# Gated mix of a long convolution and an MLP mixer on one core: fewer filter matmuls, norm arithmetic on VectorE, shift copies as transfers, and another instruction order

## The chip, the core and the metric

The kernel runs on one core of one Trainium2 chip. A core has five engines that work side by side, each through its own list of instructions in a fixed order: TensorE (PE, matrix products into PSUM; its weight loads are PEld), VectorE (DVE, element by element), ScalarE (ACT, functions, and most copies out of PSUM), GpSimd (POOL, small arithmetic and the issue of accumulating transfers) and SyncE (SP, which issues most transfers). Instructions wait on semaphores for results of other engines and of transfers. The metric is the time of one execution in microseconds (us); lower is better.

## The reference

All tensors are bf16; q, k, v are 1 x 2048 x 640.

```python
x = A_q
g = sigmoid((x * gate_w).sum(-1, keepdims=True))
# a: shift convolution of k with 4 taps per channel, times v, then a causal
#    convolution over 2048 steps with the filter ssm_k (by FFT), plus kv * ssm_D, times q
kv = k_shift * v
y  = irfft(rfft(pad(kv)) * rfft(pad(ssm_k)))[:S] + kv * ssm_D
a  = q * y
# b: layernorm, w1, gelu, a shift of four channel groups by 1, -1, 2, -2 rows, w2, residual;
#    layernorm, w3 (640 -> 1536), gelu, w4 (1536 -> 640), residual
h  = gelu(layernorm(x) @ w1)
x1 = x + shifted(h) @ w2
b  = x1 + gelu(layernorm(x1) @ w3) @ w4
return g * a + (1 - g) * b
```

## The kernel before

Sequence rows are worked on in 16 tiles of 128, in four groups (`sc`) of four tiles. The long convolution is cut in four blocks of 512 steps. Each block goes to the frequency domain by a matrix product with a discrete Fourier transform that is folded by symmetry: a signal and its reverse are added and subtracted first, so that each half needs a smaller matrix.

- **Filter** (`h_load`, `h_fold`, `h_chunk`; lines 762 to 797), five chunks of 128 channels. `h_fold` has ScalarE copy the second half of a chunk backwards into `krev`, VectorE subtract and add it (two operations of 1024 elements), and two DMA transposes (issued by SyncE) turn the result into `het`. `h_chunk` multiplies with the constant `Rh` (and `Zn`, which repairs single rows): for four groups of bins `j`, with a real and an imaginary half `r`, in all 20 matmuls of 512 columns per chunk. Even bins are `j` 0 and 1, odd bins 2 and 3. ScalarE copies the results to `HF`.
- **Signal** (`kv_block`, `x_fwd`, `combine`): VectorE makes the shifted product kv, TensorE transforms it, the result lies in `XF`.
- **Products** (`unit`): VectorE multiplies `XF` and `HF` over block pairs, in operations of 2560 elements; some sums go through accumulating transfers that GpSimd issues.
- **First norm and w1** (`ln1`, `bn_math`, `mm1`): statistics on VectorE, small arithmetic on VectorE or GpSimd, the power -0.5 on GpSimd (`pool_pow`). Of the five channel groups that `mm1` yields, the last holds 32 channels of each shift group; VectorE copies them by 32 partitions to their shifted place in `hT` (line 924).
- **w2 and second norm** (`mm2`, `ln2`, `ln_math`): for each of 16 tiles, one chain of [128 x 1] operations on GpSimd with one on VectorE (lines 868 to 873). Tiles below `LNA` are normed by VectorE, the others by ScalarE. A DMA transpose follows.
- **w3, w4** (`mm3`, `mm4`, `base`): `mm4` adds its residual by an identity matmul, unless `summed` says that the tile's row is written first (`base`) and added to in DRAM.
- **End** (`final`): the inverse transform for 16 pairs of tiles, `k` 0 to 15. For `k` below `KACC` the result is added in DRAM by an accumulating transfer from GpSimd; otherwise VectorE adds the mixer's tile and SyncE writes the sum.

Every operation is recorded in program order (`Prog.op`, `Prog.dma`; `tt`, `ts`, `act`, `mm` at lines 668 to 690 are the helpers whose line numbers the profile shows). A list written out by hand, `SEQUENCE`, gives the order in which they go to their engines. `schedule` walks it with planned durations, chooses PSUM banks as it goes, and lets large loads wait for an earlier transfer when the plan has too many under way. Waits then follow from the reads and writes. One operation of an engine waits for earlier results of the same engine too, except on TensorE.

Of the kernel before, what the change touches and what calls it, by code (L numbers as in the profile page):

```python
# [7 lines left out]
U16 = mybir.dt.uint16  # L8
# [165 lines left out]
class Prog:  # L174
# [51 lines left out]
    def dma(self, queue, out, in_, bias=0.0, transpose=False, slow=False, free=None, early=False, accum=False, fn=None):  # L226
# [12 lines left out]
        op = Op(len(self.ops), queue, [fn], [in_], [out], issue, bias, n * esz)  # L239
# [31 lines left out]
    def schedule(self, sequence, backlog=3000.0):  # L271
        ops = self.ops
        delays = self.edges()
        free = {"pe": 1580.0, "act": 720.0, "dve": 930.0, "pool": 1190.0, "sp": 720.0}
        dfree = 0.0
        done = []
        avail = [0.0] * 8
        tenant = [None] * 8
        todo = {t.idx: len(t.users) for t in self.banks}
        last = {t.idx: 0.0 for t in self.banks}  # L280
        order = []
        for i in sequence:
            o = ops[i]
            st = max([free[o.eng]] + [ops[p].end + d for p, d in delays[i]])
            if o.nbytes and not o.tp and not o.early:
                st = max(st, dfree - backlog)
            t = o.tile
            if t is not None and t.place is None:
                free_at = {b: max(avail[b:b + t.n]) for b in range(0, 8, t.n)}
                st = max(st, min(free_at.values()))  # L290
                assert st < 1e17, "no bank"
                t.place = min((avail[b ^ 1] <= st if t.n == 1 else False, a, b) for b, a in free_at.items() if a <= st)[2]
                for b in range(t.place, t.place + t.n):
                    if tenant[b] is not None:
                        for u in tenant[b].users:
                            if ops[u].eng != "pe":
                                o.preds.setdefault(u, False)
                    tenant[b] = t
                    avail[b] = 1e18
            o.start = st  # L300
            free[o.eng] = st + o.dur
            o.end = st + o.dur
            if o.nbytes:
                dfree = max(st + 0.5 * o.dur, dfree) + o.cost
                o.end = max(dfree, o.end) + o.lat
                if o.cost > 500 and not o.tp and not o.early:
                    gate = [(ops[d].end, d) for d in done if ops[d].end <= st]
                    if gate:
                        o.preds.setdefault(max(gate, key=lambda g: g[0])[1], False)
                done.append(i)  # L310
            if t is not None:
                todo[t.idx] -= 1
                last[t.idx] = max(last[t.idx], o.end)
                if todo[t.idx] == 0:
                    for b in range(t.place, t.place + t.n):
                        avail[b] = last[t.idx] + 195.0
# [112 lines left out]
def _folded_dft():  # L429
# [13 lines left out]
    no = np.stack([p, p + 128])  # L443
    ne = np.where(no == 0, 256, no)
    Rh = np.stack([np.cos(w * 2 * k * ne),
                   np.where(k == 0, no == 0, -np.sin(w * 2 * k * no)),
                   np.cos(w * (2 * ko + 1) * no),
                   -np.sin(w * (2 * ko + 1) * ne)])
    Z = np.zeros((3, 128, 128))
    Z[:2, :, 0] = ((-1.) ** ne)[:, :, 0]  # L450
    Z[2, 0] = 1.
# [6 lines left out]
    Rh = Rh.transpose(2, 0, 1, 3)  # L458
    G = G.reshape(2, 2, 2, 128, 256).transpose(3, 0, 2, 1, 4)
    return (R, np.concatenate([Rh.reshape(128, 2048), Z.transpose(1, 0, 2).reshape(128, 384)], 1),  # L460
            G.reshape(128, 8 * 256))
# [725 lines left out]
```

## Time and profile before

| | us |
|---|---|
| runs | 234.76, 235.43, 236.32 |
| median | 235.43 |
| span of the profiled execution | 233.8 |
| granted TensorE clock, mean | 0.994 of full speed |
| ScalarE busy | 170.3 |
| GpSimd busy | 105.9 |

The span runs from the first to the last instruction of one profiled execution; the times of the runs hold a little more. In rows of groups stand the line of the kernel, the engine, the operation with its output and inputs, the shape, and the count; behind the bar the time in which at least one of them ran, the mean duration of one in ns, and the engine's idle time just before them with what ended it. Rows of windows give, for each stretch, the busy time of each engine (with the number of instructions), the granted clock, the share of the transfer engines and their rate. A matmul's duration in the trace holds its way through the array, and neighbours overlap.

### The profile page before, as it was taken

The numbers are of one execution on the slowest core, as the hardware profiler recorded it, in microseconds if no ns is written. First come the engines' busy times: TensorE is split into PE (matmuls) and PEld (weight loads), VectorE is DVE, ScalarE is ACT, GpSimd is POOL, SyncE is SP. The second block draws the span as 40 slices with busy tenths as digits, with TensorE's granted clock in tenths as the row PEclk, the third lists the DMA queues.
The fourth block names the chain that finished last, engine by engine and source line by source line (L and its number), as shares of the span: only waits on it lengthen the run. The fifth ranks groups of instructions, "written<-read, shape, count | busy, mean of one in ns | idle before, by whom it ended". The sixth has DMA issues, their size and how long they took to land.

```text
span 233.8 us, 4171 instructions
## 1 busy us (share of the span) xinstructions
PE 221.1 (95%) x1501; PEld 134.6 (58%) x1501; DVE 220.1 (94%) x402; ACT 170.3 (73%) x317; POOL 105.9 (45%) x122
## 2 busy tenths in 40 slices
PE   7999999989998999999999999999999999999960
PEld 2598665436554656544775456654666556776630
DVE  6998999999988999998999999999989999979994
ACT  2799699488796899769949897577655387288881
POOL 0330406274495801196376693246024332456870
PEclk9999999999999999999999999999999999999997
DMA  5999959898878999978638988999978987989998
GB/s 161 360 345 250 253 146 271 246 277 204 140 181 176 240 213 317 343 212 180 157 97 145 187 189 163 146 191 206 259 142 145 196 140 142 185 98 111 95 109 165
DMA packets 63785, 45.48 MB, mean 195 GB/s; under 512 B 28818, under 2 KB 59028, under 8 KB 63764
## 3 DMA queue, kind: packets, MB, share of 16 engines
q1 hardware_dynamic: 54748, 33.33, 55.2%
q0 software_dynamic: 8832, 11.80, 34.9%
q8 instruction: 12, 0.20, 0.3%
q10 hardware_dynamic: 184, 0.08, 0.1%
q14 instruction: 9, 0.07, 0.1%
HBM read 24.22 MB, written 6.55 MB: 132 GB/s over the span
## 4 chain that ended last, share of the span: by engine, by line
PE 45%; DVE 9%; POOL 3%; ACT 2%; issue 1%
PE PSall L689 45%; DVE arena L669 8%; ACT arena L679 2%; POOL arena L674 1%; POOL arena L861 1%; POOL arena L669 1%; DVE arena L959 0%; DVE arena L674 0%
## 5 line engine op out<-in xcount | busy, mean ns | idle before, releaser
L689 PE MATMUL PSall<-arena 128*128 128x320 bf16 (+5 forms) x1444 | 213.7, 307 | 5.3 <-DVE arena L669 2.4
L669 DVE TENSOR_TENSOR arena<-arena 128x640 bf16<-128x640 bf16 (+5 forms) x247 | 182.3, 793 | 3.0 <-ACT arena L679 1.9
L689 PEld LDWEIGHTS PSall<-arena 128*128 128x128 bf16 (+1 forms) x1444 | 130.5, 98 | 86.9 <-DVE arena L669 4.2
L679 ACT ACTIVATE arena<-PSall 128x512 bf16<-128x512 f32 (+6 forms) x189 | 107.7, 634 | 29.4 <-PE PSall L689 25.2
L679 ACT ACTIVATE arena<-arena 128x640 bf16<-128x640 bf16 (+4 forms) x62 | 42.2, 703 | 6.7 <-POOL arena L669 2.7
L861 POOL TENSOR_TENSOR arena<-arena 128x1 f32<-128x1 f32 (+1 forms) x26 | 29.3, 1128 | 31.9 <-DVE arena L674 31.5
L674 POOL TENSOR_SCALAR arena<-arena 128x1 f32<-128x1 f32 (+2 forms) x41 | 24.8, 608 | 34.7 <-DVE arena L959 12.0
L237 POOL DMA_DIRECT2D out_dram<-arena x28 | 30.5, 1197 | 20.5 <-ACT arena L679 15.0
L679 ACT ACTIVATE arena<-PSall,arena 128x640 bf16<-128x640 f32 (+1 forms) x32 | 20.6, 658 | 20.0 <-PE PSall L689 19.9
L237 POOL DMA_DIRECT2D arena<-arena x12 | 14.9, 1242 | 32.1 <-DVE arena L669 28.2
L674 DVE TENSOR_SCALAR arena<-arena 128x640 bf16<-128x640 bf16 (+2 forms) x49 | 14.4, 307 | 3.4 <-POOL arena L674 1.6
L857 DVE BATCH_NORM_STATS2 arena<-arena 128x6 f32<-128x320 bf16 x32 | 14.6, 479 | 2.0 <-DMA arena<-in_A_q_dram 1.7
L669 POOL TENSOR_TENSOR arena<-arena 128x1 f32<-128x1 f32 (+1 forms) x11 | 10.3, 943 | 2.9 <-DVE arena L674 2.5
L715 PE MATMUL PSall<-arena 128*128 128x512 bf16 x15 | 5.4, 536 | 1.6 <-DVE arena L711 1.6
L959 DVE SCALAR_TENSOR_TENSOR arena<-PSall,arena 128x640 bf16<-128x640 f32 x8 | 6.4, 808 | 0.1
L924 DVE TENSOR_SCALAR arena<-arena 32x256 bf16<-32x256 bf16 (+1 forms) x24 | 5.9, 244 | 0.5
L679 ACT ACTIVATE PSall<-PSall 128x640 f32<-128x640 f32 x8 | 5.6, 699 | 0.1
L715 PEld LDWEIGHTS PSall<-arena 128*128 128x128 bf16 x15 | 1.9, 132 | 4.6 <-issue 2.5
L903 PE MATMUL PSall<-arena 128*128 128x128 bf16 x40 | 3.6, 219 | 0.3
L718 ACT ACT_TABLE_LOAD x1 | 1.3, 1283 | 2.7 <-issue 2.7
L903 PEld LDWEIGHTS PSall<-arena 128*128 128x128 bf16 x40 | 2.4, 97 | 1.4 <-DVE arena L858 0.4
L858 DVE BATCH_NORM_AGGREGATE arena<-arena 128x2 f32<-128x12 f32 x16 | 3.0, 197 | 0.0
(24 smaller groups left out, 9.6 us busy)
## 6 DMA issues: line engine op xcount, KB each, us to landing
arena<-arena POOLq DMA_DIRECT2D x12, 640.0 KB, 6.3
arena<-in_A_k_dram SPq DMA_DIRECT2D x14, 400.0 KB, 4.1
arena<-in_A_q_dram SPq DMA_DIRECT2D x14, 320.0 KB, 6.9
out_dram<-arena POOLq DMA_DIRECT2D x20, 160.0 KB, 4.2
arena<-in_A_ssm_k_dram SPq DMA_DIRECT2D x5, 512.0 KB, 4.4
arena<-in_A_v_dram SPq DMA_DIRECT2D x16, 160.0 KB, 3.9
arena<-in_B_w_dram SPq DMA_DIRECT2D x1, 1920.0 KB, 8.8
out_dram<-arena SPq DMA_DIRECT2D x10, 160.0 KB, 3.7
```

The lines of the kernel that those rows point to most:

```text
L237: fn = lambda e: e.dma_start(out, in_, **kw)
L669: P.op(eng, lambda e: e.tensor_tensor(o, real(a), real(b), op), [a, b], [o], dve_ns(o, [a, b], 2) if eng == "dve" else 500)
L674: P.op(eng, lambda e: e.tensor_scalar(o, real(a), s1, s2, op0=op0, **({} if op1 is None else {"op1": op1})), [a] + aps, [o], dve_ns(o, [a] ...
L679: P.op("act", lambda e: e.activation(real(o), real(a), f, bias=bias, scale=scale, **({"accum_out": accum} if accum is not None else {})), ...
L689: fns.append(lambda e, l=l, r=r, i=i: e.matmul(real(o), l, r, start=(i == 0), stop=(i == last)))
L715: P.op("pe", lambda e: e.matmul(real(pw), warm[:, 0:128], warm[:, 128:640], start=True, stop=True), [warm], [pw], 427.0 if i < 14 else 216.0)
L857: P.op("dve", lambda e, o=o, i=i: e.bn_stats(o, i), [i], [o], 400)
L858: P.op("dve", lambda e: e.bn_aggr(bna[:, t, :], bns[k]), [bns[k]], [bna[:, t, :]], 120)
L861: P.op("pool", lambda g: g.tensor_tensor(o, a, e, ALU.pow), [a, e], [o], dur)
L903: P.op("pe", [lambda e, c=c, pb=pb, xn=xn: e.transpose(real(pb)[:, 128 * c:128 * (c + 1)], xn[:, 128 * c:128 * (c + 1)], ident) for c in r ...
L924: P.op("dve", lambda e, o=hT[q, 4, c0:c0 + n], i=hx[q, :]: e.tensor_scalar(o, i, 1.0, None, op0=ALU.mult), [hx[q, :]], [hT[q, 4, c0:c0 + n ...
L959: P.op("dve", lambda e: e.scalar_tensor_tensor(x, real(pr), 1.0, x, op0=ALU.mult, op1=ALU.add, accum_out=st[1, 0][:, t:t + 1]), [pr, x], [ ...
```

## The change

- The filter's even bins are folded a second time. `h_fold` no longer uses a reversed copy: VectorE adds and subtracts across the two halves and reads one operand backwards. A new step `h_even` on VectorE (and one copy on ScalarE) adds and subtracts the halves of the transposed filter into `evn`, of which there is one buffer. `h_chunk` needs 14 matmuls for 20; the constant has 1792 columns for 2432.
- The small arithmetic of both norms and of the gate moves from GpSimd to VectorE; in the second norm it is done for 4, 4, 4, 2 and 2 tiles at a time. The power stays on GpSimd. `LNA` goes from 8 to 4.
- The 32-channel shift copies of row groups 1 to 3 become transfers that SyncE issues; `after` makes a copy wait for the one that wrote the column beside it.
- `KACC` goes from 12 to 8.
- `SEQUENCE` is another order; the PSUM banks (`PLACES`) and the waits of transfers for earlier transfers (`GATES`, 59 pairs) are now lists.
- The planned cost of VectorE operations that read backwards no longer differs. `LNS`, a limit from which ScalarE would take the first norm's sums, is 16, so that no tile uses it.

```diff
-    def schedule(self, sequence, backlog=3000.0):
+    def schedule(self, sequence, places, gates):
...
+        for d, g in gates:
+            ops[d].preds.setdefault(g, False)
...
-                t.place = min((avail[b ^ 1] <= st if t.n == 1 else False, a, b) for b, a in free_at.items() if a <= st)[2]
+                t.place = places[t.idx]
...
+    evn = V(oXF + 14336, 2048).rearrange("p (o e b c) -> p o e b c", o=2, e=2, b=4)
...
     def h_fold(c):
-        k, kr, fo = kst[c % 2], krev[c % 2], kfo[c % 2]
+        k, fo = kst[c % 2], kfo[c % 2]
         tt(k[:, 0, 0:1], k[:, 0, 0:1], Dcol[:, c:c + 1], ALU.add)
-        act(kr[:, :, 1:256], k[:, :, 511:256:-1], ACTF.Copy)
-        tt(fo[:, 1], k[:, :, 0:256], kr, ALU.subtract)
-        tt(fo[:, 0], k[:, :, 0:256], kr, ALU.add)
-        ts(fo[:, 0, :, 0:1], k[:, :, 256:257], 1.0, None, ALU.mult)
+        kh = k.rearrange("p b (h i) -> p b h i", h=2)
+        fh = fo.rearrange("p e b (h i) -> p e b h i", h=2)
+        for e, op in ((0, ALU.add), (1, ALU.subtract)):
+            tt(fh[:, e, :, :, 1:128], kh[:, :, :, 1:128], kh[:, :, ::-1, 255:128:-1], op)
+            tt(fo[:, e, :, 128], k[:, :, 384], k[:, :, 128], op)
+        ts(fo[:, :, :, 0], kh.rearrange("p b h i -> p h b i")[:, ::-1, :, 0], 1.0, None, ALU.mult)
...
+    def h_even(c):
+        ev = het[c % 2]
+        tt(evn[:, 0], ev[:, :, :, 0], ev[:, :, :, 1], ALU.add)
+        tt(evn[:, 1], ev[:, :, :, 0], ev[:, :, :, 1], ALU.subtract)
+        tt(evn[0:1, 0, 0], ev[0:1, 1, :, 0], ev[0:1, 0, :, 0], ALU.add)
+        tt(evn[0:1, 1, 0], ev[0:1, 1, :, 0], ev[0:1, 0, :, 0], ALU.subtract)
+        act(evn[0:1, :, 1], ev[0:1, :, :, 1], ACTF.Copy)
...
-                y = 2 * (j // 2) + r
-                eo = (0, 1, 1, 0)[y]
-                m = j % 2
-                pairs = [(Rh[:, y, kk, 128 * m:128 * (m + 1)], ev[:, eo, :, kk, :]) for kk in range(2)]
-                if y == 0:
-                    pairs.append((Zn[:, 2, :], ev[:, 1, :, 0, :]))
-                if j == 0 and r == 1:
-                    pairs += [(Zn[:, kk, :], ev[:, 0, :, kk, :]) for kk in range(2)]
+                if j == 0:
+                    pairs = [(Re_h[:, 2 * r], evn[:, 0, r]), (Re_h[:, 2 * r + 1], evn[:, 0, 1 - r])]
+                elif j == 1:
+                    pairs = [(Re_h[:, 4 + r], evn[:, 1, r])]
+                else:
+                    m = j % 2
+                    pairs = [(Ro_h[:, r, kk, 128 * m:128 * (m + 1)], ev[:, 1 - r, :, kk, :]) for kk in range(2)]
...
-            ts(st[0, 3][:, a:b], bna[:, a:b, 1], 1e-5, None, ALU.add, eng="dve" if a < 4 else "pool")
+                ts(st[0, 3][:, a:b], bna[:, a:b, 1], 1e-5, None, ALU.add)
...
-    def ln_math(l, t):
-        s = {f: st[l, f][:, t:t + 1] for f in range(6)}
-        ts(s[2], s[0], -1.0 / D, None, ALU.mult, eng="pool")
-        ts(s[4], s[2], s[2], 1e-5, ALU.mult, ALU.subtract, eng="pool")
-        ts(s[3], s[1], s[4], None, ALU.subtract)
-        pool_pow(s[5], s[3], neghalf[:, t:t + 1])
+    def var_of(l, a, b):
+        s = {f: st[l, f][:, a:b] for f in (0, 1, 3, 4)}
+        tt(s[4], s[0], s[0], ALU.mult)
+        ts(s[4], s[4], 1.0 / D ** 2, 1e-5, ALU.mult, ALU.subtract)
+        tt(s[3], s[1], s[4], ALU.subtract)
+    def ln_math(l, a, b):
+        var_of(l, a, b)
+        pool_pow(st[l, 5][:, a:b], st[l, 3][:, a:b], neghalf[:, a:b])
+        ts(st[l, 2][:, a:b], st[l, 0][:, a:b], -1.0 / D, None, ALU.mult)
+        if a >= LNA:
+            tt(st[l, 4][:, a:b], st[l, 2][:, a:b], st[l, 5][:, a:b], ALU.mult)
...
+                    if sc:
+                        P.dma(sp, hT[q, 4, c0:c0 + n], hx[q, :], after=[hT[q, 4, c0 - 1:c0]])
+                        continue
...
-    KACC = 12
+    KACC = 8
...
-    for t in range(12):
-        at(mm2, t)
-        at(ln2, t)
...
+    for a, b in ((0, 4), (4, 8), (8, 12), (12, 14), (14, 16)):
+        for t in range(a, b):
+            at(mm2, t)
+        at(ln2, a, b)
+        if b == 12:
+            at(w3_load)
+            at(mm3, 0)
```

## What was predicted

> **What bounds the kernel now.** I read the page first: the span, the busy times, the chain that ended last, and the groups.
>
> ```profile
> span 233.8 us, 4171 instructions
> ...
> PE 221.1 (95%) x1501; PEld 134.6 (58%) x1501; DVE 220.1 (94%) x402; ACT 170.3 (73%) x317; POOL 105.9 (45%) x122
> ...
> PE PSall L689 45%; DVE arena L669 8%; ACT arena L679 2%; POOL arena L674 1%; POOL arena L861 1%; POOL arena L669 1%; DVE arena L959 0%; DVE arena L674 0%
> ...
> L669 DVE TENSOR_TENSOR arena<-arena 128x640 bf16<-128x640 bf16 (+5 forms) x247 | 182.3, 793 | 3.0 <-ACT arena L679 1.9
> ...
> L674 DVE TENSOR_SCALAR arena<-arena 128x640 bf16<-128x640 bf16 (+2 forms) x49 | 14.4, 307 | 3.4 <-POOL arena L674 1.6
> L857 DVE BATCH_NORM_STATS2 arena<-arena 128x6 f32<-128x320 bf16 x32 | 14.6, 479 | 2.0 <-DMA arena<-in_A_q_dram 1.7
> ```
>
> TensorE and VectorE are both nearly full, 95% and 94%. The chain names TensorE (45% of the span), so a reader might stop there. But a TensorE that never idles and a VectorE that never idles look alike in a chain. The question is which of the two has time to give. I asked for the busy times by stage, and inside one dense stretch for the rows of VectorE.
>
> ```profile
> core 0: us, PE busy (x) PEld busy (x) DVE busy (x) ACT busy (x) POOL busy (x), PEclk, DMA share, GB/s
> 0.00:10.00 10.00, 8.23 (x47) 3.72 (x47) 7.13 (x33) 4.11 (x8) 2.36 (x8) 1.00 0.81 235
> 10.00:106.60 96.60, 93.64 (x696) 57.09 (x693) 92.67 (x212) 78.61 (x157) 42.80 (x59) 1.00 0.96 240
> 106.60:208.60 102.00, 101.99 (x642) 62.63 (x643) 99.12 (x106) 69.88 (x121) 46.19 (x45) 1.00 0.85 166
> 110.00:200.00 90.00, 90.00 (x564) 54.88 (x562) 88.91 (x91) 62.62 (x108) 39.88 (x39) 1.00 0.84 167
> 208.60:230.80 22.20, 17.26 (x122) 11.16 (x119) 21.20 (x54) 17.69 (x34) 14.59 (x13) 1.00 1.01 114
> 230.80:233.80 3.00, 0.00 (x0) 0.00 (x0) 0.00 (x0) 0.00 (x0) 0.00 (x0) 0.52 0.53 156
> ```
>
> ```profile
> 133.22 38.38 DVE L669 TENSOR_TENSOR arena<-arena 128x2560 bf16<-128x2560 bf16 x33
> 172.27 34.47 DVE L669 TENSOR_TENSOR arena<-arena 128x1280 bf16<-128x1280 bf16 x33 [0.67 <-ACT arena L679]
> ```
>
> ```profile
> L669 DVE TENSOR_TENSOR arena<-arena 128x2560 bf16<-128x2560 bf16 x21 | 30.0, 1485 | 0.0
> L669 DVE TENSOR_TENSOR arena<-arena 128x1280 bf16<-128x1280 bf16 x12 | 9.2, 820 | 0.0
> ```
>
> The second fence is the timeline of VectorE, the third its groups from 133.2 to 171.6. There 33 operations with no gap last 21 x 1.485 + 12 x 0.820 = 41.0 us by their own durations and take 38.4. So an operation that waits for nothing begins 0.08 us before the one ahead of it has ended. What an operation costs VectorE is its duration less 0.08.
>
> That turns the whole kernel's VectorE time into a demand. The page's rows give 247 x 0.793 + 49 x 0.307 + 32 x 0.479 = 226.2 us; the rest (statistics, shift copies, the residual on VectorE, memsets: 74 operations) I put at 19.4 from the by-form rows, an estimate. Together 245.6, less 402 x 0.08 = 32.2: **213.4 us**. The span is 20.4 longer. Of that 2.9 lie in the first 10 us (7.13 busy), 3.0 behind the last VectorE operation (the row from 230.8), and 14.5 between. From 110 to 200 VectorE idles 1.09 of 90 us while TensorE idles none: there both are the bound. The 14.5 lie mostly ahead of 106.6 and in results that a next operation waited out.
>
> **TensorE's side of the change.** The filter drops from 20 to 14 matmuls of 512 columns for each of five chunks: 30 go. KACC 12 to 8 makes `summed` false for the second half of tiles 8 to 15, so 8 identity matmuls of 320 columns come. Prices, from two windows (106.6:172, then 172:208.6) where TensorE is full:
>
> ```profile
> L689 PE MATMUL PSall<-arena 128*128 128x320 bf16 x267 | 38.3, 299 | 0.0
> L689 PE MATMUL PSall<-arena 128*128 128x512 bf16 x135 | 31.0, 379 | 0.3 <-ACT arena L679 0.3
> ...
> L689 PE MATMUL PSall<-arena 128*128 128x320 bf16 x193 | 27.0, 299 | 0.0
> L689 PE MATMUL PSall<-arena 128*128 128x512 bf16 x50 | 11.4, 379 | 0.0
> ```
>
> 267a + 135b = 65.4 and 193a + 50b = 36.6 give a = 0.132 and b = 0.224 us. TensorE saves 30 x 0.224 - 8 x 0.132 = **5.7 us**. The trace's own means (379 ns for 512) are no price, because matmuls overlap. The Trainium skill says this too (Perfetto Trace Analysis, Identifying the Most-Contended Engine: busy matmul time is a bad metric), and VectorE: DVE Perf Modes, The TRN2 errata, has max(60, 6+FD) cycles at 2.4 GHz, 0.216 us for 512, by which the saving would be an estimated 5.4; the two solved prices lie within 4% of it.
>
> **VectorE's side.** The rows that price it:
>
> ```profile
> L669 DVE TENSOR_TENSOR arena<-arena 128x640 bf16<-128x640 bf16 x80 | 36.5, 482 | 1.7 <-ACT arena L679 1.3
> L669 DVE TENSOR_TENSOR arena<-arena 128x320 bf16<-128x320 bf16 x40 | 11.6, 320 | 0.3
> L674 DVE TENSOR_SCALAR arena<-arena 128x640 bf16<-128x640 bf16 x24 | 10.2, 433 | 0.6 <-POOL arena L861 0.5
> L669 DVE TENSOR_TENSOR arena<-arena 128x1024 bf16<-128x1024 bf16 x10 | 6.7, 680 | 0.0
> L674 DVE TENSOR_SCALAR arena<-arena 128x1 f32<-128x1 f32 x20 | 3.9, 194 | 2.8 <-POOL arena L674 1.6 <-ACT arena L679 1.2
> L924 DVE TENSOR_SCALAR arena<-arena 32x256 bf16<-32x256 bf16 x16 | 3.6, 222 | 0.3
> L924 DVE TENSOR_SCALAR arena<-arena 32x512 bf16<-32x512 bf16 x8 | 2.3, 287 | 0.2
> L674 DVE TENSOR_SCALAR arena<-arena 128x4 bf16<-128x4 bf16 x5 | 0.8, 155 | 0.0
> ```
>
> - `h_even`, new: ten TENSOR_TENSORs of 1024 elements at 0.680 - 0.08 make 6.0; ten on one partition of 512 elements, at 0.42 by the line through the 320 and 640 rows, make 3.4. **+9.4**.
> - `h_fold`: two large operations before and after, now 1016 elements, one operand read backwards. No VectorE row reads backwards. Its bounds are two elements a cycle (the slope of the 640 and 320 rows: 320 elements in 0.162 us, 0.51 ns each), hence nothing, and one, hence 10 x 1016 x 0.51 ns = 5.2. I take nothing: the inner step stays one element, as in all rows at the fast slope. Two more tiny ones per chunk: +0.8.
> - The Trainium skill (Vector Engine (DVE) Microarchitecture Reference, 5.1) lets the doubled rate take steps of plus or minus one and finds no need of 4-byte alignment, but lists how a negative step streams as not measured; no trace here shows it.
> - Norm arithmetic: 16 operations of 0.194 go (-1.8); five groups bring four each and the last four groups one more, 24 at 0.155 to 0.194 (+2.3). First norm +6 (0.7), gate +6 (0.6). **+1.8**.
> - Shift copies of chunks 1 to 3 leave: 8 x 0.142 + 8 x 0.207 = **-2.8**. LNA 8 to 4: four applies leave, **-1.4**.
> - KACC: four finals (8 to 11) add the tile on VectorE, 4 x 0.402 = **+1.6**.
>
> Net **+9.4 us**, demand 222.8. If none of the some 70 new small operations overlaps its predecessor it is 15 with 0.08 x 70; with the backward read at one element 20; below 8 I see no way, since every term but the price of the tiny ones is from a row of its own kind.
>
> **The other engines.** ScalarE:
>
> ```profile
> L679 ACT ACTIVATE arena<-arena 128x640 bf16<-128x640 bf16 x32 | 25.9, 823 | 3.3 <-POOL arena L669 2.7 <-DMA arena<-arena 0.5
> L679 ACT ACTIVATE arena<-arena 1x320 bf16<-1x320 bf16 x16 | 7.1, 456 | 0.9 <-DVE arena L669 0.7
> L679 ACT ACTIVATE arena<-arena 128x1020 bf16<-128x1020 bf16 x5 | 5.3, 1065 | 2.6 <-DMA arena<-in_A_ssm_k_dram 2.5
> ```
>
> Five reversals (5.3) go, five one-partition copies of 1024 come (between 0.456 and 1.065 each; I take 1.0), four applies come (3.3), and `base` of tiles 8 to 15 halves (below 3). ScalarE stays near 171 of 230, idle enough to hide it. SyncE gains 16 shift copies and four result writes and GpSimd loses four accumulating writes:
>
> ```profile
> L237 SPq DMA_DIRECT2D out_dram<-arena x22: 332/436/1218, 113.1 to 231.1; - x22
> ```
>
> Twenty issues at 0.44 make 9 us on a queue that spreads over the whole span. Each shift copy waits in that queue for its gelu, and loads and transposes behind it wait too; the second matrix product of the tiles then waits for a landing and not for a 0.22 us copy. I count it nothing while TensorE has filter or forward-transform matmuls to run; without that cover it is a landing, some 2 to 4 us, once or twice.
>
> Two waits are added on VectorE. `off` now waits there for GpSimd's power, and the groups' arithmetic waits for ScalarE's last square. Before, GpSimd held the first and single tiles the second. At worst four powers lie bare:
>
> ```profile
> 98.47 0.75 POOL arena L861
> ...
> 99.29 0.80 POOL arena L669
> ...
> 100.18 1.36 POOL arena L674
> ...
> 101.62 1.49 POOL arena L674
> 103.12 0.76 POOL arena L861
> ```
>
> The chain of waits shows the gain on the same rows: 1.36 + 1.49 + 0.80 of GpSimd arithmetic ahead of the last tiles' norm goes, so the third product's input is ready some 3 us sooner. That is worth nothing by itself once VectorE is the bound, but it takes latency out of the stretch where the 14.5 lie. Against it, four powers at 0.75, 3.0 us of waiting for the products queued behind.
>
> **The sum.** TensorE's demand falls and VectorE's rises, so VectorE becomes the only bound: 222.8 + 2.9 + 3.0 = 228.7 us with no gap between. The forecast hangs on what is left of the 14.5. With TensorE slack, I expect VectorE to run throughout as it does from 110 to 200: of 1.09 us idle there, 0.67 was for ScalarE, itself behind TensorE, so 0.42 in 90 us, 1.0 over the kernel, and 0.5 for the last products. Span 230.2. The profile's span stands 1.6 under the median of 235.43, hence **231.8 us**. This is a bet on the new order; the rows only say that it can be done where independent products are queued.
>
> **Rivals.**
> - *VectorE full, gaps half kept* (0.22): 5 of the 14.5 stay: 233.7, 235.3 with the 1.6. No change. For it: the early part is loads, statistics and transposes, whose landings no order shortens.
> - *VectorE's queue stalls ahead of 106.6 as now* (0.23), slower: 7.8 of the 9.4 lie there, and `h_even` adds a wait for a transpose to that queue. With gaps unchanged, 233.8 + 9.4 + 1.6 = 244.8; with a third closed, 240. It decides from 5.1 us of gaps on (222.8 + 5.9 + 5.1 + 1.6 = 235.4), and is beyond 1% from 7.5.
> - *The backward read runs at one element a cycle* (0.08), slower: 231.8 + 5.2 = 237.
> - *TensorE still sets the pace* (0.10), as the chain says: 235.4 - 5.7 = 229.7. For it: VectorE's added work may fill its own idle time. Against it: that is only 13.7 us in all, 5.9 of them at the ends.
> - The forecast keeps 0.37.
>
> One per cent is about what a measurement tells from no change. Faster by over 1% (below 233.1): the forecast and TensorE's rival, 0.47. Within: 0.25, the half-kept gaps and an edge of the others. Slower: 0.28. Likeliest case alone 230 to 233; the range reaches from 229 to 240.5.
>
> **What would show it.** VectorE's busy time, by the same measure, rises by 9 while TensorE falls below 217 and shows idle time in the second half. The operations of 1016 elements last near 0.68 (at one a cycle 1.2). The idle column of VectorE from 10 to 106.6, now 3.9, says which case came: under 2, or above 5. I am wrong if VectorE's total stays at 220, or if the tail after the last matmul grows because the finals' writes come late on SyncE.

## The result, and the profile after

| | before | after |
|---|---|---|
| median of the runs, us | 235.38 (234.76 to 236.32) | 239.59 (238.65 to 239.72) |
| span of the profiled execution, us | 233.8 | 237.8 |
| granted TensorE clock, mean | 0.994 | 0.972 |

The change makes the kernel slower: the ratio is 1.0158, with a 95% interval from 1.0121 to 1.0195, or 3.7 us. Ratios leave out the runs of a kernel that took over 1.5% longer than its fastest. The forecast was 231.8. First the page of the changed kernel: its span, the busy times, the chain that ended last by engine, and its largest group of VectorE. Line numbers have moved: `mm` is L677, `tt` L657, `ts` L662, `act` L667, the power L853.

```profile
span 237.8 us, 4109 instructions
...
PE 220.9 (93%) x1479; PEld 135.5 (57%) x1479; DVE 223.8 (94%) x434; ACT 173.4 (73%) x321; POOL 64.6 (27%) x55
...
DVE 40%; PE 29%; DMA 14%; POOL 4%; SPq 4%; ACT 4%; issue 4%; DVEq 0%
...
L657 DVE TENSOR_TENSOR arena<-arena 128x640 bf16<-128x640 bf16 (+11 forms) x298 | 192.9, 721 | 8.8 <-ACT arena L667 3.8 <-DMA arena<-in_A_k_dram 2.4 <-DMA arena<-in_A_v_dram 1.7
```

The chain now holds 14% of transfers. It can't be set beside the chain of before as a whole, which was followed back only to 94.11 us; behind that time the one of the changed kernel holds a single transfer, 7.09 us from 133.09 on, and the other holds none. Next the groups by form, where the prices of the prediction are seen.

```profile
L657 DVE TENSOR_TENSOR arena<-arena 128x1016 bf16<-128x1016 bf16 x10 | 6.7, 680 | 0.1
L657 DVE TENSOR_TENSOR arena<-arena 128x1024 bf16<-128x1024 bf16 x10 | 6.5, 682 | 0.0
L657 DVE TENSOR_TENSOR arena<-arena 1x512 bf16<-1x512 bf16 x10 | 4.1, 407 | 0.0
L667 ACT ACTIVATE arena<-arena 1x1024 bf16<-1x1024 bf16 x5 | 5.2, 1043 | 0.1
```

Every one came as priced, in us: 0.682 for 0.680, 0.407 for 0.42, 1.04 for 1.0, and the backward read at 0.680, the same rate as forward. The rows of VectorE's operations sum to 258.2 us (298 x 0.721 = 214.9, the rest 43.3). Less 434 x 0.08 that is a demand of 223.5; the forecast had 222.8. So the work was sized to 0.7 us, and the time missed by 7.8.

The difference is idle time. VectorE's idle time is the span less its busy time: 13.7 us before, 14.0 after. The forecast left 7.4 of it (2.9 and 3.0 at the ends, 1.5 between). The timeline of VectorE shows where it lies; in brackets stand the idle time ahead of the row and what ended it.

```profile
48.08 1.65 DVE L657 TENSOR_TENSOR arena<-arena 128x2560 bf16<-128x2560 bf16 x3 [1.69 <-DMA arena<-in_A_k_dram]
...
85.20 1.09 DVE L657 TENSOR_TENSOR arena<-arena 128x640 bf16<-128x640 bf16 x2 [1.33 <-DMA arena<-in_A_v_dram]
...
147.76 5.91 DVE L657 TENSOR_TENSOR arena<-arena 128x2 f32<-128x2 f32 x7 [1.59 <-ACT arena L667]
155.48 20.30 DVE L657 TENSOR_TENSOR arena<-arena 128x2560 bf16<-128x2560 bf16 x20 [1.81 <-ACT arena L667]
176.38 59.31 DVE L657 TENSOR_TENSOR arena<-arena 128x2 f32<-128x2 f32 x94 [0.61 <-POOL arena L853]
```

From 176.38 on, VectorE runs 59.3 us without a gap, as the forecast expected of the whole kernel. Ahead of that stand two kinds of waits: for loads of k and v (4.1 us in all), and at 147 and 155 for ScalarE (1.59 and 1.81). Before, VectorE's waits for transfers were for q and a weight alone, and no wait for ScalarE was longer than 1.0. The timeline of all engines around the second kind (SPq is the issue of transfers by SyncE):

```profile
133.09 4.37 SPq L234 DMA_TRANSPOSE arena<-arena  x2
...
140.20 0.92 ACT L667 ACTIVATE arena<-arena 128x640 bf16<-128x640 bf16 x1 [3.20 <-DMA arena<-arena]
...
142.15 16.05 PE L677 MATMUL PSall<-arena 128*128 128x320 bf16 x101 [2.27 <-ACT arena L667]
...
146.90 0.74 ACT L667 ACTIVATE arena<-arena 128x640 bf16<-128x640 bf16 x1 [1.12 <-DMA arena<-arena]
```

ScalarE norms tiles 8 to 11 here, now as one batch of four. Each apply writes into `xn2`, of which there are two; the third apply waits 3.20 us until the transpose of the first has read its buffer, and TensorE (2.27) and VectorE (1.59) wait behind ScalarE, whose other results they need. The windows show what that costs and where else TensorE lags (the first row is for the ends); before, from 125 to 150, both engines were full (25.00 and 24.97).

```profile
0.00:10.00 10.00, 7.14 (x31) 2.70 (x31) 8.00 (x34) 3.06 (x6) 1.59 (x7) 1.00 0.80 260
...
0.00:30.00 30.00, 23.50 (x208) 16.33 (x209) 27.00 (x96) 15.86 (x39) 5.07 (x11) 0.89 1.04 255
10.00:106.60 96.60, 90.73 (x676) 57.04 (x676) 91.17 (x227) 78.27 (x150) 12.57 (x10) 0.96 0.98 229
125.00:150.00 25.00, 22.73 (x120) 11.95 (x118) 23.41 (x23) 17.79 (x34) 9.53 (x7) 0.93 0.72 136
```

VectorE's idle time from 10 to 106.6 is 5.4 us, over the 5 that the prediction named as the mark of the slower case. In the first 30 us TensorE is busy 23.50; before it was 28.00.

### The profile page after: what moved, and what is told of

It reads as the page before. It is cut to its first block, busy times and chain, and to the rows that moved or that the text cites. A ratio compares the mean times of both kernels' runs of the same rounds, so it can differ in the third digit from the quotient of the medians.

```text
span 237.8 us, 4109 instructions
## 1 busy us (share of the span) xinstructions
PE 220.9 (93%) x1479; PEld 135.5 (57%) x1479; DVE 223.8 (94%) x434; ACT 173.4 (73%) x321; POOL 64.6 (27%) x55
## 4 chain that ended last, share of the span: by engine, by line
DVE 40%; PE 29%; DMA 14%; POOL 4%; SPq 4%; ACT 4%; issue 4%; DVEq 0%
DVE arena L657 33%; PE PSall L677 28%; DMA arena<-arena 8%; DVE arena L849 4%; ACT arena L667 4%; POOL arena L853 3%; DMA arena<-in_A_v_dram 3%; SPq L237 2%; DMA arena<-in_A_k_dram 2%; SPq L234 2%; DVE arena L662 2%; DMA arena<-in_A_q_dram 1%; POOL out_dram L237 1%; DVE arena L933 1%; DVE arena L850 1%
## 5 line engine op out<-in xcount | busy, mean ns | idle before, releaser
L677 PE MATMUL PSall<-arena 128*128 128x320 bf16 (+5 forms) x1422 | 213.5, 310 | 7.9 <-ACT arena L667 4.2
L657 DVE TENSOR_TENSOR arena<-arena 128x640 bf16<-128x640 bf16 (+11 forms) x298 | 192.9, 721 | 8.8 <-ACT arena L667 3.8
L677 PEld LDWEIGHTS PSall<-arena 128*128 128x128 bf16 (+1 forms) x1422 | 131.1, 100 | 89.0 <-ACT arena L667 9.9
L667 ACT ACTIVATE arena<-PSall 128x512 bf16<-128x512 f32 (+7 forms) x189 | 109.2, 628 | 33.7 <-PE PSall L677 23.3
L667 ACT ACTIVATE arena<-arena 128x640 bf16<-128x640 bf16 (+4 forms) x66 | 43.8, 683 | 7.3 <-DMA arena<-arena 5.2
L853 POOL TENSOR_TENSOR arena<-arena 128x2 f32<-128x2 f32 (+2 forms) x15 | 26.7, 1783 | 72.0 <-DVE arena L657 43.4
L237 POOL DMA_DIRECT2D out_dram<-arena x24 | 26.2, 1254 | 52.6 <-ACT arena L667 48.3
L667 ACT ACTIVATE arena<-PSall,arena 128x640 bf16<-128x640 f32 (+1 forms) x32 | 20.4, 655 | 19.4 <-PE PSall L677 19.4
L237 POOL DMA_DIRECT2D arena<-arena x12 | 14.5, 1209 | 37.8 <-DVE arena L657 37.6
L849 DVE BATCH_NORM_STATS2 arena<-arena 128x6 f32<-128x320 bf16 x32 | 13.9, 476 | 0.9 <-DMA arena<-in_A_q_dram 0.9
L662 DVE TENSOR_SCALAR arena<-arena 128x640 bf16<-128x640 bf16 (+5 forms) x48 | 12.0, 273 | 0.1
L667 ACT ACTIVATE PSall<-PSall 128x640 f32<-128x640 f32 x8 | 5.6, 697 | 0.2
L933 DVE TENSOR_SCALAR arena<-arena 32x256 bf16<-32x256 bf16 x8 | 1.8, 219 | 1.0 <-ACT arena L667 0.9
L667 ACT ACTIVATION_READ_ACCUMULATOR arena<-PSall 128x1 f32 x8 | 1.6, 202 | 0.0
L667 ACT ACTIVATION_READ_ACCUMULATOR PSall<-PSall 128x1 f32 x8 | 1.6, 199 | 0.0
```

The source lines that it names most:

```text
L237: fn = lambda e: e.dma_start(out, in_, **kw)
L657: P.op(eng, lambda e: e.tensor_tensor(o, real(a), real(b), op), [a, b], [o], dve_ns(o, [a, b], 2) if eng == "dve" else 500)
L662: P.op(eng, lambda e: e.tensor_scalar(o, real(a), s1, s2, op0=op0, **({} if op1 is None else {"op1": op1})), [a] + aps, [o], dve_ns(o, [a] ...
L667: P.op("act", lambda e: e.activation(real(o), real(a), f, bias=bias, scale=scale, **({"accum_out": accum} if accum is not None else {})), ...
L677: fns.append(lambda e, l=l, r=r, i=i: e.matmul(real(o), l, r, start=(i == 0), stop=(i == last)))
L849: P.op("dve", lambda e, o=o, i=i: e.bn_stats(o, i), [i], [o], 400)
```

## The experiments

All were timed beside the kernel before on the same chip (its medians there: 235.2 to 235.5). Ratios are to the kernel before, with a 95% interval; the changed kernel has 1.0158 and so a difference of two ratios times 235.4 is a difference in us. Runs that leave out work, bring fewer rows or norm in place compute something else; they are there for their time alone. Line numbers differ from kernel to kernel: `tt` is L664 where `h_even` is left out, L592 where loads are early, and L608 in the last control.

### Is it the added work?

Leave out `h_even`, the change's largest addition, and let the products read the unfolded halves.

```diff
-        tt(evn[:, 0], ev[:, :, :, 0], ev[:, :, :, 1], ALU.add)
...
-                    pairs = [(Re_h[:, 2 * r], evn[:, 0, r]), (Re_h[:, 2 * r + 1], evn[:, 0, 1 - r])]
+                    pairs = [(Re_h[:, 2 * r], ev[:, r, :, 0]), (Re_h[:, 2 * r + 1], ev[:, 1 - r, :, 0])]
```

> Leaves out the second fold's arithmetic (h_even): twenty VectorE operations and one ScalarE copy per chunk group, five chunks; the 14 matmuls read the unfolded bins. Everything else, the order included, is the changed kernel's. Theory A (VectorE's demand sets the end): the twenty cost 10 x (0.68-0.08) + 10 x (0.41-0.08) = 9.3 us, and the time falls by 6 to 9 us, to 231 to 234. Theory B (the new order's late transfers and ScalarE waits set the end, VectorE has room): it falls by less than 3 us, VectorE's idle time grows by most of the 9.

Measured: 239.38 us, ratio 1.017 [1.0141, 1.0199]. VectorE lost 9.3 us of work and the kernel nothing. All of that work but one operation on one partition lies in the first 95 us, and that VectorE's demand there sets the end is refuted. Its waits for k, v and the filter grew from 4.1 to 9.5 us; the rest of the freed time went mostly into waits for TensorE (2.2), q and ScalarE.

Leave out 30 of the filter's 512-column matmuls:

```diff
-                mm(pr[:, r, :], pairs)
+                mm(pr[:, r, :], pairs[:1])
```

> Leaves out 30 more filter matmuls (8 per chunk for 14): TensorE has 30 x 0.224 = 6.7 us less to do, nothing else differs. Theory A (VectorE sets the end): no change, within 1 us. The rival of the prediction that TensorE still sets the pace: 4 to 7 us less.

Measured: 239.42, ratio 1.0182 [1.0145, 1.0218]. The filter's demand on TensorE doesn't set it either. Two engines of the same length could hide each other, so both cuts at once:

> The changed kernel with both cuts that alone changed nothing: VectorE 9.3 us less (no second fold behind the transpose) and TensorE 6.7 less (30 of the filter's 512-column products left out); the result is another one. Theory B (two engines, each as long as the other, hold each other up): only less of both shows, 231 to 234. Theories L and R (loads or transfers set the pace): still 238 to 240, with the waits for loads above the 9.5 us that the cut of VectorE alone showed.

Measured: 239.2, ratio 1.0143 [1.0102, 1.0185]. The windows up to 95 us, of the changed kernel and then of this one:

```profile
0.00:95.00 95.00, 86.27 (x647) 54.04 (x648) 87.57 (x239) 71.43 (x140) 14.17 (x16) 0.96 0.97 226
```

```profile
0.00:95.00 95.00, 80.41 (x609) 50.63 (x615) 78.33 (x218) 66.36 (x134) 14.05 (x16) 0.95 0.92 223
```

VectorE does 9.2 us less by 95 us (78.33 for 87.57), which is nearly the whole cut: with 21 operations fewer, 19 of them left out, it stands at nearly the same place of the program at that time. All of its freed time became waiting. The list of waits of the kernel with both cuts says for what (total, times, longest):

```profile
DVE arena L664 <- DMA arena<-in_A_k_dram: 3.8, 3, 2.6
DVE arena L664 <- DMA arena<-in_A_v_dram: 3.7, 3, 1.7
...
DVE arena L664 <- DMA arena<-in_A_ssm_k_dram: 1.7, 2, 0.9
```

Together 9.2 us for three loads, 5.1 more than in the changed kernel. That the sum equals the freed time is chance: of the added waiting by 95 us, 2.1 are for TensorE, and most of the rest for q and ScalarE. The time came as theories L and R had it; the waits for loads that they named (above 9.5) did not. The stretch ahead of 95 us does not follow the work of these two engines. TensorE's cut lies mostly there as well (89 matmuls of 512 columns by 95 us, for 126), so the runs say nothing on less work behind it.

### Is it the batch of four, or the listed waits?

Let tiles 10 and 11 be normed in their own place, so that no apply waits for a buffer (their residual is then the normed row):

```diff
-            x, xn, mean, rstd = X[:, t, :], xn2[t % 2], st[1, 2][:, t:t + 1], st[1, 5][:, t:t + 1]
+            x, xn, mean, rstd = X[:, t, :], X[:, t, :] if t in (10, 11) else xn2[t % 2], st[1, 2][:, t:t + 1], st[1, 5][:, t:t + 1]
```

> Tiles 10 and 11 are normed in place in X instead of in the two xn2 buffers (their residual is then the normed row), so that ScalarE need not wait for the transposes of tiles 8 and 9; order and all else as in the changed kernel. Theory C (the norms of four tiles in a row go through two buffers, ScalarE stands 3.2 us at 140, TensorE 2.3 us behind it and VectorE 1.6 and 1.8 us behind that): 2 to 4 us less. Theory A' (what comes ahead of 125 us and VectorE's dense list after 155 set the end): less than 1 us.

Measured: 237.5, ratio 1.0069 [1.0042, 1.0097]: 2.1 us less. The window says that it is this place:

```profile
125.00:150.00 25.00, 24.89 (x149) 14.54 (x150) 25.00 (x26) 19.30 (x36) 10.84 (x7) 1.00 0.80 158
```

Drop the 59 waits of transfers for transfers:

```diff
-    sched = P.schedule(SEQUENCE, PLACES, GATES)
+    sched = P.schedule(SEQUENCE, PLACES, [])
```

> The 59 written waits of transfers for earlier transfers are dropped, all else as in the changed kernel. If these waits hold loads of k and v back (VectorE idles 4.1 us for them in the changed kernel): 2 to 4 us less. If they only keep transfers from crowding each other: no change, or up to 3 us more. Theory A alone says within 1 us.

Measured: 238.21, ratio 1.0118 [1.009, 1.0146]: about 0.9 us less, but the interval overlaps that of the changed kernel, so this run alone does not show a gain. Both together:

> The changed kernel with tiles 10 and 11 normed in place and without the 59 waits of transfers for transfers. If the two are separate places (one at 133 to 156 us, the other ahead of 95), they add: 239.6 - 2.1 - 1.4 = 236.1, within 1% of before, and about 0.7 us stay for the start. If they are one time counted twice, it stays at 237.5 or above. Below 235.4 would mean that the changed work is worth something that only the order hid.

Measured: 236.94, ratio 1.0043 [1.0014, 1.0071]. By ratios the two gave 0.89% and 0.40%; together they give 1.15%. Within the intervals they add, as two separate places would; together they are 2.7 of the 3.7 us by which the changed kernel is slower. The first is shown by itself, the listed waits are not.

### Is it the shift copies as transfers?

Put the 16 copies back on VectorE, at the same places of the order:

```diff
-                    if sc:
+                    if sc > 3:
```

> The 16 late shift copies go back from SyncE transfers to VectorE, at the same places of the order. Theory A: VectorE's demand grows by 8 x 0.14 + 8 x 0.21 = 2.8 us and the time by 2 to 3 us. Theory B (the 16 issues of 0.59 us, 9.4 us of SyncE's queue between 37 and 81 us, make the loads of k and v late): 1 to 3 us less, and the idle time of VectorE ahead of k and v goes from 4.1 to under 2.

Measured: 244.12, ratio 1.035 [1.0298, 1.0401], 4.5 us slower, for 16 operations that cost VectorE 2.8. TensorE now waits for these copies in four places, 3.2 us in all. That the copies as transfers cost the time is refuted: at these places of the order they are cheaper so. Neither theory's number came (2 to 3 us more, or 1 to 3 less).

### Is it the start?

Two moves in `SEQUENCE`: two weight loads for w1 earlier, the first two chunks' folds behind the norm of the fourth tile.

> Only the order of two lists: SyncE issues the two loads of w1 right after the first tiles' loads, and VectorE does the first two chunks' folds after the fourth tile's norm. Theory D (the new order starts TensorE late: 23.5 us busy in the first 30 against 28.0, and at a clock of 0.66 from 10 to 20): 2 to 4 us less, TensorE over 26 us busy in the first 30. If the later stages set the end: less than 1 us, or the filter comes later and it is slower.

Measured: 244.02, ratio 1.0348 [1.0299, 1.0397]. The w1 loads came ahead of q's, VectorE waited 4.6 us for q, and TensorE was busy for 22.72 us by 30, where theory D had over 26 (23.50 without the edit). The edit did not make the start sooner, so it says nothing on what a sooner start is worth. With the in-place norm and without the listed waits:

> The two edits before together, and without the written waits of transfers. If each is one of several waits that bind in turn: 4 to 7 us less than the changed kernel, 232.5 to 235.5. If VectorE's demand is behind them: 2 us or less, with VectorE at over 97% busy.

Measured: 239.5, ratio 1.0158 [1.0112, 1.0203], 4.5 us below the run before and not the 232.5 to 235.5 written down. The same two edits gave 2.7 on the changed kernel's own order; the intervals are too wide to call the two gains different.

### Is it the loads?

Less to carry: 12 of the loads of k bring a fifth of the rows.

```diff
-            P.dma(sp, kt, bass.AP(A_k.tensor, k0 + (t0 - 3) * D, [[2 * D, 128], [D, 5], [1, 320]]))
+            n = 5 if u < 2 else 1
+            P.dma(sp, kt[:, 0:n], bass.AP(A_k.tensor, k0 + (t0 - 3) * D, [[2 * D, 128], [D, n], [1, 320]]))
```

> The changed kernel, but 12 of the 14 whole loads of k bring 80 KB where they brought 400 (one row in five; the rest of the buffer keeps the older rows, so the result is another one). 3.8 MB of 44 go, most of them between 30 and 115 us. Theory R: with a fifth of the bytes gone from a full stretch the time falls by 4 or more, below 235.5. Theory L: the loads land sooner by some 2 us each, VectorE's 2.4 us of waits for k go, and the time falls by 1.5 to 3. Theory B: no change beyond 1 us, other waits take the place.

Measured: 238.38 (eight runs, 235.76 to 239.61), ratio 1.0087 [1.0047, 1.0126], 1.7 us less by the ratio. That is in the range of theory L (1.5 to 3 less) and short of theory R (4 or more). VectorE's waits for k fell from 2.4 to 0.7 us, by 1.7 too, but this was profiled in the fastest run, whose span is 3.9 us shorter, so it is no proof of one to one. The loads of k lie on the path; whether by their place in the list or by their bytes is not settled, as the transfer engines' share up to 95 us fell with them, from 0.97 to 0.87.

Loads earlier in SyncE's list (30 entries of `SEQUENCE`, with the in-place norm and without the listed waits):

> The changed kernel with tiles 10 and 11 normed in place (that alone gave 237.5), without the 59 waits of transfers for transfers (that alone gave 238.2), and with 30 loads of k, v and the filter up to 60 places earlier in SyncE's list, each still behind the read that frees its buffer. Theory L (where the loads stand in that list is what VectorE waits for in the first 95 us, 4.1 us for k and v): VectorE's waits for k, v and the filter fall below 1 us, and the time falls by them below the sum of the two single edits, 236.1, to 232 to 234. Theory R (the transfer engines are full in that stretch, share 0.92 to 0.96, and an earlier issue only makes another transfer late): waits move to other transfers, 235.5 to 238. Theory B (TensorE and VectorE hold each other up through results, loads fill the idle time that is there anyway): waits for loads fall and waits for ScalarE or TensorE take their place, 235.5 to 237.

Measured: 252.6, ratio 1.0753 [1.071, 1.0796]. All theories missed. The waits for k and v were gone, as theory L said, but the first entries of VectorE's and of SyncE's lists of waits show what came for them:

```profile
DVE arena L592 <- DMA arena<-arena: 10.7, 2, 6.9
```

```profile
SPq L237 <- DVE arena L592: 81.9, 29, 25.5
```

SyncE's transfers wait 81.9 us for VectorE (35.4 in the changed kernel, and some 25 of each is one wait at the end; from 40 to 80 us it is 13.7 for 0.4): an early load stands at the head of the list until its buffer is read out, and the transposes behind it stand too. VectorE then waits 6.9 us at a stretch for a transpose. The granted clock of TensorE fell as well, to 0.89 over the first 95 us (0.96 in the changed kernel); how the added time divides between the two was not measured.

> The kernel of h1_loads_early without the second fold's work behind the transpose (the filter's products take unfolded halves, so the result is another one; VectorE does 9.3 us less). Beside h1_loads_early it says whether VectorE's added work costs anything once the loads are early. Theory L: 5 to 9 us below h1_loads_early, 225 to 229. Theory R: within 2 us of h1_loads_early. Theory B: within 2 us as well, with TensorE's idle time unchanged.

Measured: 254.04, ratio 1.0788 [1.0753, 1.0823]. Again 9.3 us less of VectorE's work made nothing faster; theories R and B had said so.

Issue the loads of v and the shift copies from GpSimd:

```diff
-        P.dma(sp, vt, A_v[0, t0:t0 + 256, ds].rearrange("(p s) d -> p s d", s=2))
+        P.dma("pool", vt, A_v[0, t0:t0 + 256, ds].rearrange("(p s) d -> p s d", s=2))
...
-                        P.dma(sp, hT[q, 4, c0:c0 + n], hx[q, :], after=[hT[q, 4, c0 - 1:c0]])
+                        P.dma("pool", hT[q, 4, c0:c0 + n], hx[q, :], after=[hT[q, 4, c0 - 1:c0]])
```

> The changed kernel with its 16 shift copies and the 16 loads of v issued by GpSimd, which runs 2.3 us of work between 60 and 125, and not by SyncE; nothing else moves. Theory S (SyncE's list, 26.1 of 30 us full from 30 to 60 and 28.5 of 35 from 60 to 95, with loads, transposes and copies held up behind each other, sets the pace of the first 95 us): the loads of k and the transposes go out sooner, VectorE's waits for k and v (4.1 us) fall to 1 or less, 234 to 237. Theory B (the fixed order of all lists at once; no single queue): 238 to 241. The price that speaks against it: an issue on GpSimd is costlier and lands later (4 to 6 us against 3.4 in the rows of transfers), so if the landing decides, 241 to 245.

Measured: 249.2, ratio 1.0563 [1.0497, 1.0629]. Waits for k fell to 1.0 us, as theory S had it; waits for v rose to 11.7, and no theory's time came. Timeline of GpSimd, then of VectorE:

```profile
90.90 1.21 POOL L853 TENSOR_TENSOR arena<-arena 128x4 f32<-128x4 f32 x1 [9.07 <-DVE arena L657]
92.08 1.50 POOL L237 DMA_DIRECT2D arena<-in_A_v_dram  x2
```

```profile
97.41 2.50 DVE L657 TENSOR_TENSOR arena<-arena 128x640 bf16<-128x640 bf16 x3 [6.11 <-DMA arena<-in_A_v_dram]
```

GpSimd had nothing to do, and still the load of v went out at 92.08: ahead of it in the list stood a power that waited 9.07 us for VectorE's norm arithmetic. 5.3 us after the issue VectorE could go on. The median landing (3.9 us for these loads, 3.4 from SyncE) explains little; the place behind the power explains this wait, 6.11 of the 11.7. What lay behind the other waits for v is not shown. The same with both cuts:

> The same with VectorE's and TensorE's work cut as in h4_less_both (no second fold behind the transpose, 30 matmuls left out; the result is another one). With 9.3 us less of VectorE, 6.7 less of TensorE and 18 us of issues off SyncE, theory S gives 228 to 233. Theory B: 237 to 240 as in h4_less_both, 239.2. If the landings on GpSimd's queue decide: above 240, with VectorE waiting for v more than the 3.7 us of h4_less_both.

Measured: 243.8, ratio 1.0375 [1.0308, 1.0441]. Here less work does show, 4.4 us by the ratios. Of the three cases written down the third came: above 240, with VectorE waiting 9.5 us for v. That the landings are the reason, as it says, is not shown by that.

### Is it the order?

Four programs with orders made anew, all by the same local search, which starts from the order of the kernel before and goes by the planned durations of its `schedule`; neither `PLACES` nor `GATES`. The first has the whole change, the second only the second fold, the third all but the fold, the last is the kernel before, its work unchanged.

```diff
-    SEQUENCE = [1, 4, 3, 6, ...
+    SEQUENCE = [...
```

> All of the change's work, but in an order made from that of the kernel before: new operations set in behind what they need, then shifted about by a search on the planner of the kernel before, which also picks the banks again (no PLACES, no GATES). Theory O (the new order and its waits lose the time, the work doesn't): within 1% of the kernel before, 233 to 237.5. Theory W (10 us more for VectorE must show in any order): 238 to 243.

> Only the second fold (14 matmuls, h_even, the backward read) is added to the kernel before, order made in the same way. By VectorE's demand (+9.4 +0.8) and TensorE's saving (6.7): theory W says 3 to 8 us slower than before, 238 to 243; if the fold pays for itself: within 1 us of before or faster.

> All parts but the second fold (20 matmuls, ScalarE's reversal): batched norms on VectorE, shift copies as transfers, KACC 8, LNA 4, order made in the same way. VectorE's demand is 1 us under that of the kernel before, TensorE's 1 us over it. Theory W: 233 to 236. If the batched norms and the transfers are what loses: 237 or more.

> The kernel before with nothing changed but its order, made by the same search: what a search of this kind does by itself. Its plan is 0.2% shorter: 234 to 237; over 237.5 would say that the orders of the three others are worse than the one written out, whatever their work.

| | us | ratio |
|---|---|---|
| all parts | 243.58 | 1.0327 [1.0279, 1.0376] |
| fold alone | 244.06 | 1.0371 [1.0321, 1.0421] |
| all but the fold | 243.94 | 1.0347 [1.0296, 1.0398] |
| kernel before, order made anew | 245.01 | 1.0403 [1.0363, 1.0443] |

The last row is the control: the same instructions as before, by its plan 0.2% shorter than the order of the kernel before, run 4% slower. Against it the whole change is 0.8% faster, the fold alone 0.3% and the rest 0.6%, each by one order, and all three intervals overlap the control's. So these four say little on the parts of the change: as written down for the control, above 237.5 the made orders are worse than the written one whatever their work. Nor do they say what the changed kernel's own order costs, since the kernel before was not run in that order. The windows from 125 to 180 us of the kernel before, of the control, and two rows of the control's VectorE:

```profile
125.00:180.00 55.00, 55.00 (x333) 32.36 (x332) 54.30 (x50) 39.58 (x69) 24.17 (x22) 1.00 0.92 181
```

```profile
125.00:180.00 55.00, 48.36 (x284) 27.12 (x282) 47.72 (x47) 35.65 (x65) 28.64 (x25) 1.00 0.79 157
```

```profile
152.38 0.21 DVE L613 TENSOR_SCALAR arena<-arena 128x1 f32<-128x1 f32 x1 [2.69 <-POOL arena L613]
157.38 69.75 DVE L608 TENSOR_TENSOR arena<-arena 128x2560 bf16<-128x2560 bf16 x77 [3.40 <-DMA arena<-arena]
```

6.6 of its 8.9 us of longer span are lost here, in waits for the norm's arithmetic on GpSimd and for a transfer: the stretch of the second norm, where the changed kernel loses 2.1 as well.

## Why the prediction was wrong

- **The step that failed** is the one on gaps: "With TensorE slack, I expect VectorE to run throughout as it does from 110 to 200", 1.5 us left of 14.5. Counted as there (span less demand and ends), 237.8 - 223.5 - 2.0 - 2.1 = 10.2 were left (2.0 idle in the first 10 us, and 2.1 behind the last operation, which ends at 176.38 + 59.31). The 14.5 had been two things. By its rows VectorE's 402 operations sum to 245.5 us and its busy time was 220.1, so they overlapped by 25.4 and not by the 32.2 that I took off: 6.8 us were dependent operations that did not overlap, and 7.7 were idle. The first kind did go (258.2 - 223.8 = 34.4, for 34.7 taken off), which the prediction had not told apart; so VectorE's busy time rose by 3.7 and not by the 9 that it named as a sign, though the rows hold 12.7 more. The idle kind grew to 9.9. Over the whole span it was waiting for loads of q, k and v (5.0) and for ScalarE (4.7), and 6.7 us less of TensorE's work made nothing faster.
- **VectorE as the only bound**: the sizes were right and the role was wrong. The runs with 9.3 us less of VectorE, 6.7 less of TensorE and both say that neither sets the time ahead of 95 us, where most of the 9.4 was to be paid. A page with 94% busy looked like a bound; there it is an engine that meets its loads just as they land, and in the changed order some 4 us after it could have used them. In the last 59.3 us VectorE does run without a gap, and its rows there have 20 operations of 640 elements, for 16 in the kernel before from 172.2 on: the four finals of KACC, priced at 1.6 us. What they cost was not tested.
- **The rival that came nearest in time**, gaps ahead of 106.6 kept and a third closed (240), had the right number: a third is what closed, and the idle time from 10 to 106.6 was 5.4. But its price, 9.4 us of added work in that stretch, is refuted by the run without it. A sum that comes out is no evidence for its terms. The rival called half kept had a third in its sum, 5 of 14.5; with the 10.2 that did stay the same sum gives 240.5.
- **ScalarE** was called "idle enough to hide" four more applies. It was idle enough, but the four tiles of a batch share two buffers, and that wait, which the diff shows in `for a, b in ((0, 4), ...)`, was not looked for: 2.1 us.
- **Listed waits of transfers** were not priced: 0.9 us by the ratio, which noise could make.
- **Shift copies** were rightly a gain as transfers; the bared powers came to 0.61 us of waiting where 3.0 was the bound; TensorE's saving of 5.7, most of it in the filter ahead of 95 us, could not show, since 6.7 more does not either. Its busy time (220.9, forecast below 217) did not fall, partly for a reason of the clock told below.
- **What stays open**: the last 1.0 us, for which the four finals are a candidate; what a sooner start is worth (the one edit for it brought another wait); and what sets the pace of the first 95 us as a whole. Fewer bytes of k count 1.7 us there by the ratio, and moving loads to another place in a queue or to another queue made it worse both times, with long waits for what then stood behind or ahead. No version here beats the kernel before; the best, 236.94, is 0.4% above it, and with another result.

## What to carry to other kernels

Before an engine at 94% is called the bound, take work away from it: if the time stays, the engine is, in the stretch that the work came from, only where the waits end, and what it costs to add or cut there is not the price on its rows. In a list that issues in order, an instruction is as late as whatever stands ahead of it and holds up whatever stands behind: ask of each load not when its queue is free but what the entry ahead waits for, and of each batch how many buffers its members share. And where a change brings a new order with it, time the old work under an order made the same way; here one such order alone moved the time by 4%, more than the whole change did. Such a control serves only programs whose order was made in the same way: here the three beside it, not the changed kernel.

## What the hardware showed beside it

TensorE's clock. In the changed kernel TensorE waits 3.14 us for VectorE early on, by its timeline:

```profile
13.18 0.71 PE L909 MATMUL PSall<-arena 128*128 128x128 bf16 x5 [3.14 <-DVE arena L662]
```

Then it runs at little over half speed. The windows of the changed kernel and then of the kernel before (the clock is the third number from the end):

```profile
12.00:16.00 4.00, 2.45 (x21) 2.03 (x22) 4.00 (x18) 1.26 (x4) 0.00 (x0) 0.59 1.10 328
16.00:20.00 4.00, 4.00 (x48) 3.98 (x49) 4.00 (x14) 1.27 (x5) 1.41 (x2) 0.56 1.64 221
```

```profile
12.00:16.00 4.00, 3.98 (x78) 3.67 (x76) 3.91 (x16) 3.73 (x11) 1.66 (x3) 1.00 1.08 352
16.00:20.00 4.00, 4.00 (x60) 3.63 (x58) 3.40 (x11) 4.00 (x12) 0.00 (x0) 1.00 1.21 324
```

4 x 0.41 + 4 x 0.44 = 3.4 us of full speed are lost, and "busy" in the row from 16 to 20 hides it: 4.00 of 4.00 busy, with 48 matmuls for 60. What they cost in time no run shows. The Trainium skill (TensorE: Matmul & The Clock Gate, Part 1) has the array fall to half its clock after an idle window of about 3.4 us and rise again after a busy one. The half agrees: from 13.18 to 18.00 the granted clock was 0.50. The length does not: the wait was 3.14, and a shorter one, 2.27 us ahead of 142.15, was enough as well (0.60 and 0.55 from 142 to 146). At that place the length alone does not decide: behind 2.02 us the clock fell with the copies on VectorE (0.86 over 140 to 150), behind 2.37 with both cuts it stayed at 1.00.

GpSimd beside VectorE. The same power on 128 x 2 elements took 0.70 us in the first norm, with VectorE mostly on statistics, and 8.61 in the second, while VectorE ran products without a pause:

```profile
16.54 0.70 POOL L853 TENSOR_TENSOR arena<-arena 128x2 f32<-128x2 f32 x1 [5.17 <-DVE arena L662]
...
167.74 8.61 POOL L853 TENSOR_TENSOR arena<-arena 128x2 f32<-128x2 f32 x1
```

It ended as VectorE ran out of work and waited, 0.61 us, for just this result. The Trainium skill (GPSIMD Engine Reference, 1. Specifications) says that GpSimd shares its way to SBUF with VectorE and contends with its operations of two SBUF inputs; this row fits that, and no run here took the products away to show it.
